# Attention feeding a two-layer network: normalising and transposing of late pairs started by the network's gates, and one chunk normalised on two engines

## The chip, the cores and the metric

One core of a Trainium2 chip runs the whole program. Its engines work side by side and are tied by semaphores: TensorE (PE), VectorE (DVE), ScalarE (ACT), GpSimd (POOL), and SyncE (SP), which here only issues transfers. The metric is the device time of one execution in microseconds, as the median of several runs.

## What is computed

Causal attention by blocks of 64 positions, then a two-layer network on its output, all in float32 (cut):

```python
scores = scale * np.matmul(q, k.transpose(0, 1, 3, 2))       # 8 batches, 8 heads, 576 positions, 64 per head
scores = np.where(block_i >= block_j, scores, -1000000000.0)
attn = np.exp(scores - np.max(scores, axis=-1, keepdims=True))
attn = attn / (np.sum(attn, axis=-1, keepdims=True) + 1e-09)
x = np.matmul(attn, v)                                       # then reshaped to 4608 tokens x 512
h = x @ w_in                                                 # 512 -> 2048
return (h * (1.0 / (1.0 + np.exp(-1.702 * h)))) @ w_out      # 2048 -> 512
```

## The kernel before

**Attention.** Two heads are done together as a pair; there are 32 pairs, n = 0 to 31, four to a batch. The queries of a pair are cut into five chunks, i = 0 (64 queries) and 1 to 4 (128 each). Chunk i sees 64(2i+1) keys. For each chunk and head, `score` puts the scores in a PSUM bank (matmuls `bank<-qk` in early pairs, `bank<-high`, `bank<-high,low` and `bank<-low,high` in late ones). `weigh` adds the mask and takes the maximum on DVE (L448, `e<-bank`), then the exponential on ACT (L455), with the sum in `sm`. `normalise` makes the reciprocal on DVE (L464, L469) and multiplies `e` by it for each head, on POOL (L474), or for chunk 4 of late pairs on DVE (L476). `turn` (late pairs) transposes `e` on DVE in blocks of 32 into `turned`: the blocks left of the diagonal by one instruction a head (L483), and the diagonal blocks of both heads by one (L488, called the diagonal turn here; in the profile 64x128, in the program's order 64x2x2x32). After chunk 4's turn, 16 transfers on SP's queue put the parts of `turned` in their places (L495). `av` multiplies by the values on PE (`bank<-turned,vp`) and ACT copies the result to `xr` (L574, L575). In early pairs (n < 8) `flip` does the transposing with PE (L117) and ACT instead.

`prep` readies q and k of the next pair: two transposes on DVE (L332, to `qt` and `raw`), two roundings on ACT (L333, `high`), and the remainders on POOL (`low`, L88).

**The network.** Tokens are done in 12 tiles of 384. A tile has 16 gates. A gate is 12 matmuls into the bank `hp`, then `tanh` on ACT (`g<-hp`, L692), the product on DVE (`g<-g,hp`, L693), its rounding on ACT (`gh`, L701), and the remainder on POOL (`gl`, L88); then come the nine matmuls of the gate before it into three accumulators `acc`, six on `gh` (`woh`, `wol`) and three on `gl`. There is one buffer `g`, so the next `tanh` waits for this `gl`. At a tile's start `split` rounds `xr` to `xh` on ACT (L626) and makes `xl` on DVE. At its end ACT copies each `acc` to `osb` (L658) and issues its transfer.

**Order.** `ORDER` gives for each pair a row of slots: digits are the chunks that are scored, V is `av` of the pair before, N normalises and T turns the chunks that were weighed, L is `prep`. Matmuls of the network fill in between the slots by a quota. HANDOVER is the row of pair 8, FIRST_LATE that of pair 9. In a late pair V also scores chunk 4 of the running pair. After its weighing, `settle` calls `prep` of the next pair, and normalises and turns chunk 4. The recording layer sorts each engine's instructions; those marked with `tc.keep_in_program_order` keep their place among each other, and `tc.high_priority` draws a gate's instructions forward.

**The lent bank.** Late, gates take two PSUM banks in turn for `hp`. The one that is not in use is lent to the first score matmul of a pair and to chunk 4, and the gate behind a loan uses the same bank as the gate ahead of it:

```python
def next_hp():
    if turns["late"] and not gate_bank["lent"]:
        gate_bank["now"], gate_bank["spare"] = gate_bank["spare"], gate_bank["now"]
    gate_bank["lent"] = False
    return ps.tile([P, 512], F32, tag=gate_bank["now"], name="hp")
```

So the first score matmul of a pair, `bank<-high 64x64`, writes the bank from which the gate before the last read its `hp`.

Of the kernel before, what the change touches and what calls it, by code (L numbers as in the profile page):

```python
# [14 lines left out]
ALU = mybir.AluOpType  # L15
# [10 lines left out]
ORDER = (  # L26
# [3 lines left out]
)  # L30

START = "1+0 - B 2/3 L C - V - 4 - a - - -"
HANDOVER = "B C - 0+3/2+1 - - N - T - V - L - - -"
FIRST_LATE = "0+3/2+1 - - N - - T - - V - - -"


WEIGHTS_BY = ((0, 0), (8, 13), (14.5, 32))
# [4 lines left out]
def attention_moe_kernel(  # L42
# [9 lines left out]
    nc = tc.nc  # L52
# [20 lines left out]
    def f(ap):  # L73
        return ap.bitcast(F32)
# [115 lines left out]
    def width(i):  # L190
        return BLK * (2 * i + 1)
# [208 lines left out]
    def settle(n, banks, todo):  # L400
        for chunks, part in zip(banks, todo):
            e = {}
            for i, hd, lo, hi, s in part:
                if i not in e:
                    e[i] = es[i] if early(n) else weights_of(n, i)
                weigh(n, i, hd, lo, hi, s, e[i])
            if early(n):
                for i in chunks[::-1]:
                    if n == 2 * HP - 1 and i == NCH - 1:
                        with tc.high_priority(offset=300):  # L410
                            normalise(n, i, e[i])
                    else:
                        normalise(n, i, e[i])
            else:
                weighed.extend((n, i, e[i]) for i in chunks[::-1])
            if 4 in chunks and not early(n):
                if n + 1 < NPAIR and n != 2 * HP:
                    prep(n + 1)
                normalise_all()
                turn_all()  # L420

    weighed = []
    shared = {}

    def weights_of(n, i):
# [3 lines left out]
            shared[n] = d2.tile([P, 2, S], F32, tag="e0", name="e", bufs=1)  # L429
        return shared[n][:, :, BLK * i * i : BLK * (i + 1) * (i + 1)]  # L430

    def normalise_all():
        for x in weighed:
            normalise(*x)

    def turn_all():
        for x in weighed:
            turn(*x)
        weighed.clear()

    def weigh(n, i, hd, lo, hi, s, e):
        mx, sm = stats[n]
# [14 lines left out]
                bias=mx[0:m, i, hd : hd + 1], accum_out=sm[0:m, i, hd : hd + 1],  # L457
            )

    def normalise(n, i, e):  # L460
        _, sm = stats[n]
        m = BLK if i == 0 else P
        c = sm[0:m, i]
        x = nc.vector.tensor_scalar(  # L464
            out=c, in0=c, scalar1=1e-9, scalar2=2.0, op0=ALU.add, op1=ALU.mult
        )
        if not early(n) and i == NCH - 1:
            tc.keep_in_program_order(x)
        nc.vector.reciprocal(out=c, in_=c)  # L469
        on = SCALE_ON[phase(n)][i]  # L470
        for hd in range(2):
            x, sc = e[0:m, hd], c[:, hd : hd + 1]
            if on == "P":
                nc.gpsimd.tensor_tensor(out=x, in0=x, in1=sc.to_broadcast([m, width(i)]), op=ALU.mult)  # L474
            elif on == "D":
                nc.vector.tensor_scalar(out=x, in0=x, scalar1=sc, scalar2=None, op0=ALU.mult)  # L476
            else:
                nc.scalar.activation(out=x, in_=x, func=AF.Copy, scale=sc)

    def turn(n, i, e):  # L480

        for hd in range(2 if i else 0):
            nc.vector.transpose(  # L483
                out=tw[:, :, SLOT[i] : SLOT[i] + i, hd].rearrange("p b j c -> p j b c"),
                in_=e[:, hd, 0 : i * P],
            )
        r, half = slice(BLK, P) if i else slice(0, BLK), slice(2, 4) if i > 2 else slice(0, 2)
        nc.vector.transpose(  # L488
            out=tw[r, half, DIAG[i]].rearrange("p b h c -> p h b c"), in_=e[r, :, i * P : width(i)]
        )  # L490
        if i == NCH - 1:
            for kb in range(4):
                for qb in range(4):
                    ns = NT4 if qb > 1 else 10 if kb > 1 else 11
                    nc.sync.dma_start(  # L495
                        out=pw[kb * 32 : kb * 32 + 32, qb, 0:ns], in_=tw[qb * 32 : qb * 32 + 32, kb, 0:ns]
                    )
# [92 lines left out]
    def step(n):  # L590

        turns["n"] = n
        now = n < NPAIR

        def item(x):
            if x == "V":
                return (lambda: av(n - 1)) if n else None
            if x in ("N", "T"):
                return normalise_all if x == "N" else turn_all
            if x == "L":  # L600
                return (lambda: prep(n + 1)) if n + 1 < NPAIR else None
            if x in ("a", "B", "C"):
                m, chunks = {"a": (n, [0, 1]), "B": (n - 1, [2, 3]), "C": (n - 1, [4])}[x]
                return (lambda: flip(m, chunks)) if m >= 0 else None
            return (lambda: score(n, [[int(z) for z in y.split("+")] for y in x.split("/")])) if now and x != "-" else None

        return [item(x) for x in order(n)]
# [29 lines left out]
    def moe():  # L637
        prev = None

        def second(state):  # L640
            g_hi, g_lo, fc, acc, t = state
            todo = [(c, ga, wb) for c in range(TILES[t][1] // P) for ga, wb in ((g_hi, "woh"), (g_hi, "wol"), (g_lo, "woh"))]
            if fc < NFC - 1:

                todo.sort(key=lambda x: (fc == 0 and x[0] == 2, x[1] is g_lo))
            elif t == NT - 1:
                todo.sort(key=lambda x: (x[0] == 2, x[1] is g_lo))
            begun = set()
            for x, (c, ga, wb) in enumerate(todo):
                last = ga is g_lo  # L650
                mm(
                    out=acc[c], lhsT=ga[:, c * P : (c + 1) * P], rhs=weights(wb, fc // FG)[:, fc % FG],
                    start=fc == 0 and c not in begun, stop=fc == NFC - 1 and last,
                )
                begun.add(c)
                if fc == NFC - 1 and last:
                    osb = out_room([P, DM], F32, "osb", t == NT - 1)
                    nc.scalar.copy(out=osb, in_=acc[c])  # L658
                    r = TILES[t][0] + c * P
                    tc.keep_in_program_order(nc.scalar.dma_start(out=out[r : r + P, :], in_=osb))  # L660
                if x % 3 == 2:
                    yield 650

        for t in range(NT):
            tt = TILES[t][1]
            if t == 0:
                yield ("tile", 0)
                split(0)
            xh, xl = xs["xh"], xs["xl"]
            acc = [ps.tile([P, DM], F32, tag=f"acc{c}", name=f"acc{c}") for c in range(tt // P)]  # L670
            for fc in range(NFC):
                if t == 0:
                    convert(fc // FG * GROUP + NDC + fc % FG + 1)
                hp = next_hp()
                fs = slice(fc % FG * P, (fc % FG + 1) * P)
                terms = [(wa, xb, dc) for dc in range(NDC) for wa, xb in (("wih", xh), ("wil", xh), ("wih", xl))]
                if fc == 0:

                    terms.sort(key=lambda x: x[1] is xl)
                for cnt, (wa, xb, dc) in enumerate(terms):  # L680
                    mm(
                        out=hp[:, 0:tt], lhsT=weights(wa, fc // FG)[:, dc, fs], rhs=xb[:, dc, 0:tt],
                        start=cnt == 0, stop=cnt == 3 * NDC - 1,
                    )
                    if cnt % 3 == 2:
                        yield unit1(tt)
                g = d2.tile([P, TT], F32, tag="g", name="g", bufs=1)[:, 0:tt]
                gh = d2.tile([P, TT], F32R, tag="gh", name="gh")[:, 0:tt]
                gl = d2.tile([P, TT], F32R, tag="gl", name="gl")[:, 0:tt]

                with tc.high_priority(offset=300):
                    nc.scalar.activation(out=g, in_=hp[:, 0:tt], func=AF.Tanh, scale=1.702)  # L692
                    nc.vector.scalar_tensor_tensor(  # L693
                        out=g, in0=g, scalar=1.0, in1=hp[:, 0:tt], op0=ALU.add, op1=ALU.mult
                    )

                if fc == NFC - 1 and t + 1 < NT:
                    yield ("tile", t + 1)
                    split(t + 1)
                with tc.high_priority(offset=300):  # L700
                    nc.scalar.copy(out=gh, in_=g)  # L701
                    subtract(nc.gpsimd, gl, g, f(gh))
                yield ("gate", fc)
                if prev is not None:
                    yield from second(prev)
                prev = (gh, gl, fc, acc, t)
        yield from second(prev)
# [87 lines left out]
```

## Time and profile before

| | |
|---|---|
| runs | 1100.33, 1099.47, 1097.53 us; median 1099.47 |
| profiled execution | 1097.42 us, span 1095.6 us |
| mean granted clock of TensorE | 0.989 |
| busy PE, DVE, ACT, POOL | 1055.2, 596.1, 521.7, 477.1 us |

The page cuts the span in 40 slices of 27 us. In its second part PE's row reads 5, 8 and 6 tenths in the first three slices and 9 in nearly all later ones: the early pairs are alone at first, then the network runs with them, and from about 930 us it runs alone. A row of a timeline has the start in us, the duration in us, the engine, the line, the operation, what it writes and reads, the count of merged instructions, and in brackets the idle time before it with what ended it. A row of waits has the waiting engine and line, what released it, the total in us, how often, and the longest. A row of windows has the stretch, its length, the busy time of PE, weight loads, DVE, ACT and POOL, the granted clock, and the transfers' share.

### The profile page before, as it was taken

What the parts mean: (1) busy time and instruction counts of PE and PEld (TensorE: products, weight loads), DVE (VectorE), ACT (ScalarE), POOL (GpSimd) and SP (SyncE); (2) the same over time, 40 slices, a digit from 0 to 9 for tenths busy, and PEclk for the clock granted to TensorE, in tenths of its full rate; (3) what the DMA queues carried; (4) which work ended last, traced back from release to release, by engine and by line L of the source; (5) the groups of instructions that cost most, each with busy time, mean ns of one, the idle gap of its engine ahead of it and who ended that gap; (6) DMA issues with size and microseconds to landing.
All of it is one profiled execution on the core that took longest, in us unless ns stands there. A gap on an engine that the chain in (4) does not pass through costs nothing. (4 is left out here: it accounts for less than half of the span.)

```text
span 1095.6 us, 20658 instructions
## 1 busy us (share of the span) xinstructions
PE 1055.2 (96%) x7236; PEld 920.8 (84%) x7236; DVE 596.1 (54%) x1856; ACT 521.7 (48%) x1367; POOL 477.1 (44%) x601
## 2 busy tenths in 40 slices
PE   5869999999999999999999999999999999999998
PEld 3657777888888888898888888888888888999987
DVE  6786786745654655655646655645665654211111
ACT  5866776534534544444544543543544443322322
POOL 4665565634444443444444434444444343222222
PEclk8979999999999999999999999999999999999999
DMA  9634523333334443333444343333444332200000
GB/s 181 202 91 156 145 66 81 95 59 82 101 78 87 104 102 65 87 84 72 106 87 89 84 104 63 81 93 78 107 98 89 65 82 49 56 29 1 30 1 30
DMA packets 222441, 92.08 MB, mean 84 GB/s; under 512 B 200832, under 2 KB 200832, under 8 KB 222336
## 3 DMA queue, kind: packets, MB, share of 16 engines
q1 hardware_dynamic: 212416, 80.73, 32.6%
q10 hardware_dynamic: 9920, 10.03, 2.6%
q8 instruction: 57, 0.93, 0.4%
q14 instruction: 48, 0.39, 0.1%
HBM read 45.88 MB, written 9.44 MB: 50 GB/s over the span
## 5 line engine op out<-in xcount | busy, mean ns | idle before, releaser
L88 POOL TENSOR_TENSOR gl<-g,gh 128x384 fp32r<-128x384 f32 x192 | 194.2, 1012 | 440.6 <-ACT gh L701 434.5
L693 DVE SCALAR_TENSOR_TENSOR g<-g,hp 128x384 f32<-128x384 f32 x192 | 105.3, 548 | 359.8 <-ACT g L692 359.7
L114 PE MATMUL hp<-xh,wih 128*128 128x384 f32 x768 | 261.1, 340 | 3.1 <-DVE g L693 2.4
L114 PE MATMUL hp<-xh,wil 128*128 128x384 f32 x768 | 258.7, 337 | 0.0
L114 PE MATMUL hp<-xl,wih 128*128 128x384 f32 x768 | 255.1, 339 | 0.1
L114 PE MATMUL acc<-woh,gh 128*128 128x512 f32 x576 | 232.0, 403 | 4.0 <-ACT gh L701 4.0
L114 PE MATMUL acc<-wol,gh 128*128 128x512 f32 x576 | 227.2, 394 | 0.0
L692 ACT ACTIVATE g<-hp 128x384 f32<-128x384 f32 x192 | 93.5, 487 | 250.3 <-PE hp L114 187.6
L701 ACT CAST gh<-g 128x384 fp32r<-128x384 f32 x192 | 98.5, 513 | 175.9 <-DVE g L693 175.0
L114 PE MATMUL acc<-woh,gl 128*128 128x512 f32 x576 | 170.6, 394 | 3.1 <-POOL gl L88 3.1
L114 PEld LDWEIGHTS hp<-xh,wih 128*128 128x128 f32 x768 | 144.6, 188 | 16.2 <-DVE g L693 3.3
L114 PEld LDWEIGHTS hp<-xh,wil 128*128 128x128 f32 x768 | 144.6, 188 | 7.7
L114 PEld LDWEIGHTS hp<-xl,wih 128*128 128x128 f32 x768 | 144.0, 188 | 1.4 <-DVE xl L88 1.4
L455 ACT ACTIVATE e<-e,mx 128x192 f32<-128x192 f32 (+3 forms) x240 | 132.4, 554 | 6.4 <-DVE mx L448 4.9
L114 PEld LDWEIGHTS acc<-woh,gl 128*128 128x128 f32 x576 | 107.3, 188 | 30.4 <-POOL gl L88 6.7
L114 PEld LDWEIGHTS acc<-woh,gh 128*128 128x128 f32 x576 | 108.1, 188 | 26.9 <-ACT gh L701 4.6
L474 POOL TENSOR_TENSOR e<-e,sm 128x448 f32<-128x448 f32 (+1 forms) x192 | 112.4, 612 | 35.4 <-DVE sm L469 22.4
L114 PEld LDWEIGHTS acc<-wol,gh 128*128 128x128 f32 x576 | 108.4, 188 | 17.0 <-issue 0.4
L448 DVE CUSTOM_DVE_ANT_0 e<-bank,mask 128x192 f32<-128x192 f32 (+3 forms) x240 | 93.2, 440 | 7.2 <-PE bank L114 7.0
L114 PEld LDWEIGHTS bank<-turned,vp 128*64 128x64 f32 (+1 forms) x1800 | 79.3, 136 | 13.8 <-issue 10.8
L114 PE MATMUL bank<-turned,vp 128*64 128x128 f32 (+2 forms) x1800 | 87.5, 259 | 1.6 <-ACT turned L509 1.6
L483 DVE STREAM_TRANSPOSE turned<-e 128x384 f32<-128x384 f32 (+1 forms) x192 | 84.0, 484 | 0.9 <-issue 0.2
(62 smaller groups left out, 1181.0 us busy)
## 6 DMA issues: line engine op xcount, KB each, us to landing
turned<-turned SPq DMA_DIRECT2D x192, 96.0 KB, 2.2
raw<-in_q_dram SPq DMA_DIRECT2D x128, 72.0 KB, 2.3
out_dram<-osb ACTq DMA_DIRECT2D x36, 256.0 KB, 2.4
raw<-in_k_dram SPq DMA_DIRECT2D x120, 72.0 KB, 2.4
turned<-turned SPq DMA_DIRECT2D x96, 88.0 KB, 2.1
words<-in_moe_w_in_dram SPq DMA_DIRECT2D x16, 512.0 KB, 6.0
vp<-in_v_dram SPq DMA_DIRECT2D x60, 128.0 KB, 2.6
turned<-turned SPq DMA_DIRECT2D x96, 80.0 KB, 2.1
```

What stands on the lines that cost most here:

```text
L88: eng.tensor_tensor(out=out, in0=in0, in1=in1, op=ALU.subtract)
L114: return tc.keep_in_program_order(nc.tensor.matmul(**kw))
L448: nc.vector.tensor_tensor_reduce(out=e[0:m, hd, lo:hi], in0=s, in1=mk, op0=ALU.add, op1=ALU.min, scale=-0.125, scalar=3e38 if lo == 0 else ...
L455: nc.scalar.activation(out=e[0:m, hd], in_=e[0:m, hd], func=AF.Exp, scale=-1.0, bias=mx[0:m, i, hd : hd + 1], accum_out=sm[0:m, i, hd : hd ...
L474: nc.gpsimd.tensor_tensor(out=x, in0=x, in1=sc.to_broadcast([m, width(i)]), op=ALU.mult)
L483: nc.vector.transpose(out=tw[:, :, SLOT[i] : SLOT[i] + i, hd].rearrange("p b j c -> p j b c"), in_=e[:, hd, 0 : i * P],)
L692: nc.scalar.activation(out=g, in_=hp[:, 0:tt], func=AF.Tanh, scale=1.702)
L693: nc.vector.scalar_tensor_tensor(out=g, in0=g, scalar=1.0, in1=hp[:, 0:tt], op0=ALU.add, op1=ALU.mult)
L701: nc.scalar.copy(out=gh, in_=g)
```

## The change

Before, N normalised all weighed chunks at one place and T turned them at another. Now N only notes how many there are (`begin_pace`). From then on each gate, right behind its remainder `gl`, normalises up to two chunks (`gate_scales`), and the next gate, right behind its product, turns them (`gate_turns`). What is left when chunk 4 has been weighed is done there, as before (`finish_all`). POOL's multiplications and DVE's turns that a gate hands out keep their program order. The T slots are gone. Besides, in pair 7 (the last early one) chunk 4 is normalised with head 0 on DVE and head 1 on POOL, where POOL did both. The arithmetic is the same.

```diff
@@ -26,12 +26,12 @@
 ORDER = (
     "1+0 - B 2/3 - L C - 4 - V - a -",
     "1+0 - B - 2 - C - 3 L V - a - 4 -",
-    "0+3/2+1 - N - T - - V - - - - -",
+    "0+3/2+1 - N - - - - V - - - - -",
 )
 
 START = "1+0 - B 2/3 L C - V - 4 - a - - -"
-HANDOVER = "B C - 0+3/2+1 - - N - T - V - L - - -"
-FIRST_LATE = "0+3/2+1 - - N - - T - - V - - -"
+HANDOVER = "B C - 0+3/2+1 - - N - - - V - L - - -"
+FIRST_LATE = "0+3/2+1 - - N - - - - - V - - -"
 
 
 WEIGHTS_BY = ((0, 0), (8, 13), (14.5, 32))
@@ -416,10 +416,11 @@
             if 4 in chunks and not early(n):
                 if n + 1 < NPAIR and n != 2 * HP:
                     prep(n + 1)
-                normalise_all()
-                turn_all()
+                finish_all()
 
     weighed = []
+    scaled = []
+    pace = {"left": 0}
     shared = {}
 
     def weights_of(n, i):
@@ -429,14 +430,37 @@
             shared[n] = d2.tile([P, 2, S], F32, tag="e0", name="e", bufs=1)
         return shared[n][:, :, BLK * i * i : BLK * (i + 1) * (i + 1)]
 
-    def normalise_all():
+    def pin(ins, behind):
+
+        if behind:
+            tc.keep_in_program_order(ins)
+
+    def finish_all():
+
+        pace["left"] = 0
         for x in weighed:
             normalise(*x)
-
-    def turn_all():
-        for x in weighed:
+        for x in scaled + weighed:
             turn(*x)
+        scaled.clear()
         weighed.clear()
+
+    def begin_pace():
+        pace["left"] = len(weighed)
+
+    def gate_turns():
+
+        for x in scaled:
+            turn(*x, behind=True)
+        scaled.clear()
+
+    def gate_scales():
+
+        for x in weighed[: min(2, pace["left"])]:
+            normalise(*x, behind=True)
+            weighed.remove(x)
+            scaled.append(x)
+            pace["left"] -= 1
 
     def weigh(n, i, hd, lo, hi, s, e):
         mx, sm = stats[n]
@@ -457,7 +481,7 @@
                 bias=mx[0:m, i, hd : hd + 1], accum_out=sm[0:m, i, hd : hd + 1],
             )
 
-    def normalise(n, i, e):
+    def normalise(n, i, e, behind=False):
         _, sm = stats[n]
         m = BLK if i == 0 else P
         c = sm[0:m, i]
@@ -470,24 +494,26 @@
         on = SCALE_ON[phase(n)][i]
         for hd in range(2):
             x, sc = e[0:m, hd], c[:, hd : hd + 1]
+            if n == 2 * HP - 1 and i == NCH - 1:
+                on = "DP"[hd]
             if on == "P":
-                nc.gpsimd.tensor_tensor(out=x, in0=x, in1=sc.to_broadcast([m, width(i)]), op=ALU.mult)
+                pin(nc.gpsimd.tensor_tensor(out=x, in0=x, in1=sc.to_broadcast([m, width(i)]), op=ALU.mult), behind)
             elif on == "D":
                 nc.vector.tensor_scalar(out=x, in0=x, scalar1=sc, scalar2=None, op0=ALU.mult)
             else:
                 nc.scalar.activation(out=x, in_=x, func=AF.Copy, scale=sc)
 
-    def turn(n, i, e):
+    def turn(n, i, e, behind=False):
 
         for hd in range(2 if i else 0):
-            nc.vector.transpose(
+            pin(nc.vector.transpose(
                 out=tw[:, :, SLOT[i] : SLOT[i] + i, hd].rearrange("p b j c -> p j b c"),
                 in_=e[:, hd, 0 : i * P],
-            )
+            ), behind)
         r, half = slice(BLK, P) if i else slice(0, BLK), slice(2, 4) if i > 2 else slice(0, 2)
-        nc.vector.transpose(
+        pin(nc.vector.transpose(
             out=tw[r, half, DIAG[i]].rearrange("p b h c -> p h b c"), in_=e[r, :, i * P : width(i)]
-        )
+        ), behind)
         if i == NCH - 1:
             for kb in range(4):
                 for qb in range(4):
@@ -595,8 +621,8 @@
         def item(x):
             if x == "V":
                 return (lambda: av(n - 1)) if n else None
-            if x in ("N", "T"):
-                return normalise_all if x == "N" else turn_all
+            if x == "N":
+                return begin_pace
             if x == "L":
                 return (lambda: prep(n + 1)) if n + 1 < NPAIR else None
             if x in ("a", "B", "C"):
@@ -694,12 +720,14 @@
                         out=g, in0=g, scalar=1.0, in1=hp[:, 0:tt], op0=ALU.add, op1=ALU.mult
                     )
 
+                gate_turns()
                 if fc == NFC - 1 and t + 1 < NT:
                     yield ("tile", t + 1)
                     split(t + 1)
                 with tc.high_priority(offset=300):
                     nc.scalar.copy(out=gh, in_=g)
                     subtract(nc.gpsimd, gl, g, f(gh))
+                gate_scales()
                 yield ("gate", fc)
                 if prev is not None:
                     yield from second(prev)
```

The instructions of PE and of SP stand in the same order in both programs. On ACT three places differ: at the start of a tile, the third copy `osb<-acc` now stands ahead of the `tanh` next to it.

DVE in an ordinary late pair, from the last reciprocal of the four chunks to the first weighing of chunk 4, before:

```order
L469 RECIPROCAL sm<-sm 128x2
L693 SCALAR_TENSOR_TENSOR g<-g,hp 128x384 x2
L488 STREAM_TRANSPOSE turned<-e 64x2x2x32 x2
L693 SCALAR_TENSOR_TENSOR g<-g,hp 128x384
L488 STREAM_TRANSPOSE turned<-e 64x2x2x32
L693 SCALAR_TENSOR_TENSOR g<-g,hp 128x384
L483 STREAM_TRANSPOSE turned<-e 128x3x4x32 x2
L488 STREAM_TRANSPOSE turned<-e 64x2x2x32
L483 STREAM_TRANSPOSE turned<-e 128x4x32 x2
L483 STREAM_TRANSPOSE turned<-e 128x2x4x32 x2
L332 STREAM_TRANSPOSE qt<-raw 128x576
L332 STREAM_TRANSPOSE raw<-raw 128x576
```

The same place in the changed program, whose lines have moved (L719 is the product of L693; L509 and L514 are the turns of L483 and L488):

```order
L493 RECIPROCAL sm<-sm 128x2
L719 SCALAR_TENSOR_TENSOR g<-g,hp 128x384 x4
L509 STREAM_TRANSPOSE turned<-e 128x3x4x32 x2
L514 STREAM_TRANSPOSE turned<-e 64x2x2x32 x2
L509 STREAM_TRANSPOSE turned<-e 128x4x32 x2
L514 STREAM_TRANSPOSE turned<-e 64x2x2x32
L509 STREAM_TRANSPOSE turned<-e 128x2x4x32 x2
L514 STREAM_TRANSPOSE turned<-e 64x2x2x32
L332 STREAM_TRANSPOSE qt<-raw 128x576
L332 STREAM_TRANSPOSE raw<-raw 128x576
```

Three diagonal turns that stood between the products of four gates now stand behind the fourth, ahead of `qt`; the large turns stand where they stood.

DVE in the last pair, from the same reciprocals, before:

```order
L488 STREAM_TRANSPOSE turned<-e 64x2x2x32
L469 RECIPROCAL sm<-sm 128x2
L464 TENSOR_SCALAR sm<-sm 128x2
L469 RECIPROCAL sm<-sm 128x2
L488 STREAM_TRANSPOSE turned<-e 64x2x2x32 x2
L693 SCALAR_TENSOR_TENSOR g<-g,hp 128x384 x2
L483 STREAM_TRANSPOSE turned<-e 128x3x4x32 x2
```

And now:

```order
L493 RECIPROCAL sm<-sm 128x2
L488 TENSOR_SCALAR sm<-sm 128x2
L493 RECIPROCAL sm<-sm 128x2
L719 SCALAR_TENSOR_TENSOR g<-g,hp 128x384 x3
L509 STREAM_TRANSPOSE turned<-e 128x3x4x32 x2
L514 STREAM_TRANSPOSE turned<-e 64x2x2x32 x2
```

The three diagonal turns ahead of the first product have gone behind the third. The same holds for pair 9, where `qt` and one more product stand between them and the turns of chunks 1 and 2.

POOL in an ordinary late pair, before, with `e` the scaling of chunks 3, 0, 1 and 2:

```order
L88 TENSOR_TENSOR low<-qt,high 128x288 x2
L88 TENSOR_TENSOR gl<-g,gh 128x384 x2
L474 TENSOR_TENSOR e<-e,sm 128x448 x2
L474 TENSOR_TENSOR e<-e,sm 64x64 x2
L474 TENSOR_TENSOR e<-e,sm 128x192 x2
L474 TENSOR_TENSOR e<-e,sm 128x320 x2
L88 TENSOR_TENSOR gl<-g,gh 128x384 x4
```

And now:

```order
L88 TENSOR_TENSOR low<-qt,high 128x288 x2
L88 TENSOR_TENSOR gl<-g,gh 128x384 x4
L500 TENSOR_TENSOR e<-e,sm 128x448 x2
L500 TENSOR_TENSOR e<-e,sm 64x64 x2
L88 TENSOR_TENSOR gl<-g,gh 128x384
L500 TENSOR_TENSOR e<-e,sm 128x192 x2
L500 TENSOR_TENSOR e<-e,sm 128x320 x2
```

The scaling has moved two gates back and is parted by a `gl`.

## The prediction

> **What bounds the kernel now.** I read, in this order, the page's busy times, the windows by stage, the waits of PE, and then the timelines of PE and DVE at the places named there.
>
> ```profile
> PE 1055.2 (96%) x7236; PEld 920.8 (84%) x7236; DVE 596.1 (54%) x1856; ACT 521.7 (48%) x1367; POOL 477.1 (44%) x601
> 300.00:910.00 610.00, 607.56 (x4310) 540.96 (x4309) 354.02 (x1148) 284.67 (x759) 270.97 (x354) 1.00 0.39 87
> PE bank L117 <- POOL turned L474: 4.1, 3, 2.9
> PE acc L114 <- ACT gh L701: 4.0, 2, 2.4
> PE acc L114 <- POOL gl L88: 3.1, 5, 0.8
> PE bank L114 <- DVE g L693: 0.2, 1, 0.2
> ```
>
> PE is busy 96% of the span, and between 300 and 910 us it is busy 607.56 of 610 at full granted clock. The change leaves PE's own order alone, so it can only remove waits of PE or add some. The waits that it can reach are few: `gh` 4.0, `gl` 3.1, and part of the 4.1 for `turned`. That caps any gain near 10 us. What it can add is not capped: a wait that recurs with every late pair comes about twenty times.
>
> **The two long waits, removed.** At the first late pair with a planned N (about 215 us) and the last pair (about 908 us), DVE has diagonal turns in front of `g`, and these wait for POOL's scaling.
>
> ```profile
> 215.15 0.47 ACT L692 ACTIVATE g<-hp 128x384 f32<-128x384 f32 x1
> 218.64 0.31 DVE L488 STREAM_TRANSPOSE turned<-e 64x128 f32<-64x128 f32 x1 [1.05 <-POOL e L474]
> 218.98 0.56 DVE L693 SCALAR_TENSOR_TENSOR g<-g,hp 128x384 f32<-128x384 f32 x1
> 220.13 0.50 PE L114 MATMUL acc<-woh,gh 128*128 128x512 f32 x1 [2.36 <-ACT gh L701]
> 912.46 0.50 PE L114 MATMUL acc<-woh,gh 128*128 128x512 f32 x1 [1.60 <-ACT gh L701]
> ```
>
> In the new order `g` stands ahead of all these turns, and the scaling comes behind two more `gl`. `g` then waits for `tanh` alone, which ends at 215.62, and can run some 3 us earlier; `gh`, which is 0.65 behind `g` and takes half a microsecond, comes almost 1 us ahead of PE's need at 217.8 (220.13 less the wait). Both waits go: 2.4 + 1.6, and 0.1 each because a matmul after a wait takes 0.50 us (the two PE rows) instead of the page's mean of 0.40. Gain 4.2 us; I keep 3.6 to 4.4.
>
> **The gl waits.** POOL scales all four chunks, eight instructions, ahead of one `gl` (six of them here).
>
> ```profile
> 375.98 2.83 POOL L474 TENSOR_TENSOR e<-e,sm 64x64 f32<-64x64 f32 x6 [0.36 <-DVE sm L464]
> 379.82 0.72 PE L114 MATMUL acc<-woh,gl 128*128 128x512 f32 x2 [0.77 <-POOL gl L88]
> PE acc L114 <- POOL gl L88: 0.8, 2, 0.6
> ```
>
> The last row is the waits of 200 to 300 us alone. There `gl` is late only through the scales, so those two go (0.8, with the longer matmuls 1.0). The three of 0.77 us (one every 250 us, at the start of a tile) lose this cause too, but output copies on ACT queue behind the same late `tanh`, and they free the accumulator that PE needs next; of these three I count 0.2 each. Together 1.6 us, bounds 0.8 to 3.4.
>
> **Chunk 4 of pair 7 on two engines.** POOL does both heads, 1.15 us each, and PE waits for each.
>
> ```profile
> 181.13 2.26 POOL L474 TENSOR_TENSOR turned<-turned,sm 128x576 f32<-128x576 f32 x2
> 182.34 0.33 PE L117 MATMUL bank<-ident,turned 128*128 128x128 f32 x1 [0.38 <-POOL turned L474]
> 183.44 1.20 PE L117 MATMUL bank<-ident,turned 128*128 128x128 f32 x9 [0.78 <-POOL turned L474]
> 182.51 0.70 DVE L248 TENSOR_SCALAR wm<-wm 128x512 uint32<-128x512 uint32 x1 [1.73 <-ACT wm L244]
> 458.67 1.51 DVE L476 TENSOR_SCALAR e<-e,sm 128x576 f32<-128x576 f32 x2
> 458.87 1.97 POOL L88 TENSOR_TENSOR low<-qt,high 128x288 fp32r<-128x288 f32 x2 [1.52 <-ACT high L333]
> ```
>
> One POOL instruction less ends POOL's half at 182.3 instead of 183.4. DVE's half costs about half a microsecond (two took 0.96 with POOL quiet, the row at 364.70 below). Side by side, both are ready at 182.3 and PE gains 1.1; one after the other, at 182.8, and it gains 0.65. The rows at 458 speak for a mutual delay: two such scales took 1.51 beside POOL's subtractions, and these took 1.97. I take 0.8. DVE is idle ahead of its next instruction, which waits for ACT until 182.51, so nothing behind the new scale on DVE is late by more than 0.3.
> [...]
>
> **What is moved in every late pair, and what it costs.** In an ordinary pair three of the four diagonal turns (L488) now stand between other gates' `g`, where DVE is idle. The new order puts all four behind the fourth `g`, ahead of `qt` and `raw`.
>
> ```profile
> 348.50 0.64 DVE L488 STREAM_TRANSPOSE turned<-e 64x128 f32<-64x128 f32 x2
> 352.40 0.31 DVE L488 STREAM_TRANSPOSE turned<-e 64x128 f32<-64x128 f32 x1
> 356.01 0.56 DVE L693 SCALAR_TENSOR_TENSOR g<-g,hp 128x384 f32<-128x384 f32 x1 [3.30 <-ACT g L692]
> 356.48 1.03 DVE L483 STREAM_TRANSPOSE turned<-e 128x384 f32<-128x384 f32 x2
> 357.52 0.31 DVE L488 STREAM_TRANSPOSE turned<-e 64x128 f32<-64x128 f32 x1
> 357.86 1.16 DVE L483 STREAM_TRANSPOSE turned<-e 128x128 f32<-128x128 f32 x4
> 358.94 0.73 DVE L332 STREAM_TRANSPOSE qt<-raw 128x576 f32<-128x576 f32 x1
> 360.57 0.67 ACT L333 CAST high<-raw 128x576 fp32r<-128x576 f32 x1 [3.46 <-DVE raw L332]
> 363.83 0.48 ACT L692 ACTIVATE g<-hp 128x384 f32<-128x384 f32 x1
> 364.70 0.96 DVE L476 TENSOR_SCALAR e<-e,sm 128x576 f32<-128x576 f32 x2
> 366.78 0.52 DVE L693 SCALAR_TENSOR_TENSOR g<-g,hp 128x384 f32<-128x384 f32 x1
> 367.75 0.24 PE L114 MATMUL bank<-high 64*64 64x64 f32 x2
> ```
>
> From 356.48 to 367.30 this is one chain without slack: turns, `qt`, `raw`, then ACT (`high`, two `xr` copies, `high`, two exponentials, `tanh`), then on DVE chunk 4's scale and turns, then `g`. ACT's row at 360.57 waits for DVE's `raw`, and `tanh` stands behind it in ACT's queue. So what is put ahead of `qt` moves the `g` at 366.78 by its full length. Who needs that `g`? The next pair's first score matmul (367.75) writes the lent bank, which is the one from which this `g` reads `hp`. `g` ends at 367.30: 0.45 us to spare. That the wait is real shows where a pair already has two more diagonal turns in the chain:
>
> ```profile
> 261.99 0.55 DVE L693 SCALAR_TENSOR_TENSOR g<-g,hp 128x384 f32<-128x384 f32 x1 [3.42 <-ACT g L692]
> 262.58 0.51 DVE L488 STREAM_TRANSPOSE turned<-e 64x128 f32<-64x128 f32 x2
> 265.57 0.73 DVE L332 STREAM_TRANSPOSE qt<-raw 128x576 f32<-128x576 f32 x1
> 273.41 0.52 DVE L693 SCALAR_TENSOR_TENSOR g<-g,hp 128x384 f32<-128x384 f32 x1
> 273.98 0.24 PE L114 MATMUL bank<-high 64*64 64x64 f32 x2 [0.17 <-DVE g L693]
> ```
>
> Here `qt` starts 3.58 us after the gate's `g`, there 2.93: 0.65 for two turns, 0.33 each. PE waited, and started 0.05 after `g` ended; so the usable slack is 0.40. Three turns more cost 3 x 0.33 = 0.98 at the least. At the most they cost 0.42 each, 1.26, since two of them now part large turns that overlap today (the two of 0.55 each at 356.48 take 1.03 together): 0.08 more each, an estimate. I take 1.1, so PE waits 1.1 - 0.4 = 0.7 per pair (0.58 to 0.86).
>
> ```profile
> L114 PE MATMUL bank<-high 64*64 64x64 f32 x40 | 4.9, 240 | 0.0
> 456.75 1.02 DVE L88 TENSOR_TENSOR xl<-xr,xh 128x384 fp32r<-128x384 f32 x1
> 457.23 1.04 PE L114 MATMUL hp<-xl,wih 128*128 128x384 f32 x4
> ```
>
> The first row counts these matmuls between 300 and 905 us: 40, two per pair, so 20 pairs, none of which waits today. In 18 of them the price is 0.7, 12.6 us. In two (458 and 708 us) a tile starts within the chain: `xl` ends at 457.77, when PE is at the last of four matmuls that read it. There the whole 1.1 falls on PE, 2.2 us. The pair at 262 us gets one turn more: 0.4. Loss 15.2 us, bounds 12.7 to 18.5. The other moved steps are covered: each half of the scaling (under the 2.83 us that six of the eight take) fits behind a `gl` and ahead of the next, since the gates there are some 4 us apart (348.50, 352.40, 356.01); by that spacing `e` is scaled about 1.7 us before DVE turns it. The DMAs of `turned` on SP's queue are issued 1.1 later and are needed only at the next pair's V, more than half of a pair's 30 us on (20 pairs in 600 us). Three times ACT puts one output copy ahead of a `tanh`, just before a V, whose matmuls hide it.
>
> **The sum.** -4.2 - 1.6 - 0.8 + 15.2 = +8.6 us. The profiled execution took 1097.42 us (span 1095.6 and 1.8 around it), which becomes 1106.0. The median shown, 1099.47, is 2.05 above that execution; with it I forecast 1108.1 us, 0.8% slower. A change under 0.3% (3.3 us) can't be told from none here.
>
> **Rivals.**
> - Faster: the chain does not reach PE, because the delay is taken up before the `g` at 366.78. That needs a total shift of at most 0.4 us. Then the gains stand alone: 1099.5 - 6.6 = 1092.9. For it: the 18 matmuls wait for nothing today. Against it: 0.33 per turn is read in the same chain, and at 273.98 the wait appears with two turns more. Chance 0.10.
> - No change: the turns overlap better than taken, as the two at 262.58 that took 0.51 together (0.26 each). Shift 0.8: 18 x 0.4 + 2 x 0.8 + 0.3 = 9.1, less 6.6, is +2.5: 1102.0. Chance 0.11.
> - Slower still: the turns of chunks 1 and 2 wait for POOL's scaling, since it now comes a gate before them. They have about 1.7 us to spare; each microsecond beyond costs 20 us: 1128 for one. Against it, POOL has nothing else between those gates. Chance 0.05.
> - The forecast: 0.74, own range 1104 to 1113.
>
> The range 1101 to 1113 takes in the no-change case and leaves the outer two. Slower 0.79, same 0.11, faster 0.10.
>
> **What the new profile would show.** Right: about 18 waits of PE on DVE's `g` at `bank<-high 64x64`, 0.5 to 0.9 us each, with `g` at that place some 1.1 us later after its pair's V; two waits on `xl`; no wait of PE for `gh` over 1 us; at most one short wait on POOL near 182 us. Wrong: no waits on `g`, and PE busy over 608 of 610 us in the late pairs. I would be most wrong if the distance from the fourth `g` to `qt` did not grow from 2.9 to about 4 us, or if waits on POOL's scaling appeared ahead of DVE's turns.

## The result: 1.2% slower

| | before | after |
|---|---|---|
| median | 1097.69 us (6 runs, 1096.58 to 1100.33) | 1111.9 us (6 runs, 1108.52 to 1113.73) |
| profiled execution, its span | 1097.42, 1095.6 | 1112.06, 1110.3 |
| mean granted clock | 0.989 | 0.989 |

The ratio is 1.0123 (95% interval 1.0102 to 1.0144): 14.2 us by the medians and 14.7 by the spans, where the sum gave 8.6. The forecast of 1108.1 us is only 3.8 below the median of 1111.9, but 1.8 of that nearness is luck: it was counted from 1099.47, the median of the first three runs of before, and all six give 1097.69. First the page's busy times, the window of the late pairs, three rows of PE's waits, and the group of the matmul that was to wait, from 300 to 930 us (its last column is the idle time ahead of it), all of the changed kernel:

```profile
PE 1057.0 (95%) x7236; PEld 919.9 (83%) x7236; DVE 590.2 (53%) x1857; ACT 521.1 (47%) x1367; POOL 477.7 (43%) x600
300.00:910.00 610.00, 590.75 (x4192) 523.08 (x4191) 337.54 (x1101) 271.95 (x724) 261.38 (x338) 1.00 0.38 85
PE bank L114 <- DVE g L719: 16.6, 19, 2.3
PE hp L114 <- ACT xh L652: 2.8, 2, 1.4
PE acc L114 <- ACT osb L684: 1.1, 3, 0.4
L114 PE MATMUL bank<-high 64*64 64x64 f32 x40 | 5.0, 244 | 16.0 <-DVE g L719 16.0
```

PE is busy 590.75 us of 610 in the late pairs, where it was 607.56. The waits on `gh` and `gl` are gone from the table of waits; in their place PE waits 16.6 us on DVE's `g` at the first score matmul, nineteen times (18 of them, 16.0 us, within the last row's window). One ordinary pair, DVE and then PE:

```profile
353.59 0.56 DVE L719 SCALAR_TENSOR_TENSOR g<-g,hp 128x384 f32<-128x384 f32 x1 [3.64 <-ACT g L718]
354.06 1.03 DVE L509 STREAM_TRANSPOSE turned<-e 128x384 f32<-128x384 f32 x2
355.11 0.64 DVE L514 STREAM_TRANSPOSE turned<-e 64x128 f32<-64x128 f32 x2
356.15 0.31 DVE L514 STREAM_TRANSPOSE turned<-e 64x128 f32<-64x128 f32 x1
357.26 0.31 DVE L514 STREAM_TRANSPOSE turned<-e 64x128 f32<-64x128 f32 x1
357.60 0.78 DVE L332 STREAM_TRANSPOSE qt<-raw 128x576 f32<-128x576 f32 x1
365.48 0.52 DVE L719 SCALAR_TENSOR_TENSOR g<-g,hp 128x384 f32<-128x384 f32 x1
366.06 0.24 PE L114 MATMUL bank<-high 64*64 64x64 f32 x2 [0.66 <-DVE g L719]
```

From the fourth `g` to `qt` it is now 4.01 us (357.60 less 353.59), where it was 2.93: all four diagonal turns stand there. The `g` that ends the chain ends at 366.00, and PE, which has been ready for 0.66, starts at 366.06.

Because PE runs the same instructions in the same order in both programs, the start of one matmul in both traces tells how far the changed kernel is behind at that place. What happens between two places is what the difference grows or shrinks by:

| matmul | before | after | after less before |
|---|---|---|---|
| second flip of chunk 4, pair 7 | 183.44 | 182.07 | -1.4 |
| first `woh,gh` after the first long wait | 220.13 | 216.27 | -3.9 |
| first score matmul near 262 to 274 | 273.98 | 269.72 | -4.3 |
| the next one (a tile has begun in that pair) | 305.54 | 302.38 | -3.2 |
| an ordinary one | 367.75 | 366.06 | -1.7 |
| `hp` of a tile that starts within the chain | 456.88 | 457.96 | +1.1 |
| first score matmul, a tile has begun | 555.76 | 560.65 | +4.9 |
| `hp` of a tile that starts within the chain | 706.98 | 716.25 | +9.3 |
| behind the scores of a pair in which a tile has begun | 807.90 | 821.95 | +14.1 |
| last pair's first score matmul | 900.49 | 916.96 | +16.5 |
| first `woh,gh` behind the second long wait | 912.46 | 927.16 | +14.7 |

### The profile page after: what moved, and what is told of

It is laid out like the page before. It is cut to its first block, busy times and chain, and to the rows that moved or that the text cites. A ratio compares the mean times of both kernels' runs of the same rounds, so it can differ in the third digit from the quotient of the medians.

```text
span 1110.3 us, 20530 instructions
## 1 busy us (share of the span) xinstructions
PE 1057.0 (95%) x7236; PEld 919.9 (83%) x7236; DVE 590.2 (53%) x1857; ACT 521.1 (47%) x1367; POOL 477.7 (43%) x600
## 4 chain that ended last, share of the span: by engine, by line
PE 68%; DVE 14%; ACT 9%; DMA 4%; issue 3%; POOL 1%; SPq 1%; DVEq 0%; ACTq 0%; POOLq 0%
PE hp L114 27%; PE acc L114 27%; PE bank L114 12%; DVE turned L509 4%; ACT e L479 3%; DMA vp<-in_v_dram 2%; DVE e L502 1%; ACT high L333 1%; DVE g L719 1%; DVE sm L488 1%; DVE turned L514 1%; DMA out_dram<-osb 1%; ACT turned L479 1%; PE bank L117 1%; DVE wm L259 1%
## 5 line engine op out<-in xcount | busy, mean ns | idle before, releaser
L719 DVE SCALAR_TENSOR_TENSOR g<-g,hp 128x384 f32<-128x384 f32 x192 | 105.4, 549 | 379.1 <-ACT g L718 379.0
L509 DVE STREAM_TRANSPOSE turned<-e 128x384 f32<-128x384 f32 (+1 forms) x192 | 85.6, 482 | 0.7 <-issue 0.3
```

What stands on the lines that cost most here:

```text
L509: pin(nc.vector.transpose(out=tw[:, :, SLOT[i] : SLOT[i] + i, hd].rearrange("p b j c -> p j b c"), in_=e[:, hd, 0 : i * P],), behind)
L719: nc.vector.scalar_tensor_tensor(out=g, in0=g, scalar=1.0, in1=hp[:, 0:tt], op0=ALU.add, op1=ALU.mult)
```

## The experiments

The theory is the prediction's: what stands on DVE between the fourth `g` and `qt` reaches PE through the lent bank. Its rival is POOL: that the scaling, handed out later, is what makes things late. For the three pairs with far longer waits (1.5 to 2.3 us, beside 0.66) the changed kernel's trace suggested a second cause, the output copy on ACT.

**1. Lending another bank.** Every engine runs the same instructions in the same order as in the changed kernel; only the bank that a gate last read is given to the fourth scores of a pair instead of the first.

```diff
-  ss.append(lent_bank() if taken == 1 and turns["late"] else bank())
+  ss.append(lent_bank() if taken == 4 and turns["late"] else bank())
```

> The changed kernel, but the lent bank goes to the fourth bank of a pair's scores and not to the first; the instructions of all engines stand in the same order, only the banks differ. Theory (PE waits because the first score matmul writes the bank from which g still reads): the bank is written some 0.9 us later, the waits of 0.65 us vanish, the three large ones shrink by 0.9, those on xh stay: 1112 - 16 x 0.73 - 2.7 - 0.4 = about 1097. Rival (PE would wait there anyway, for scores' inputs or weights that come late with the same chain): another wait of the same length appears in its place, 1112.

Measured: 1097.6 us (ratio to before 1.000, 0.9991 to 1.0009), 14.3 less than the changed kernel. The same group, from 250 to 930 us, of this kernel:

```profile
L114 PE MATMUL bank<-high 64*64 64x64 f32 x42 | 5.1, 240 | 0.0
```

So the waits at the first score matmul (16.0 us in all in the changed kernel's row) come from its write to the bank from which `g` reads: DVE's order is that of the changed kernel, and PE no longer waits there. The rival's second wait did not appear in the ordinary pairs. What is left of waits on `g` from 295 to 920 us of this kernel:

```profile
PE bank L114 <- DVE g L719: 1.7, 3, 1.0
PE hp L114 <- DVE g L719: 1.7, 3, 0.6
```

The first are the three longer pairs, at the fourth bank, which 0.9 us more could not cover; the second are three new ones at the `hp` of a gate (368, 622 and 876 us).

**2. Diagonal turns released.** The changed kernel, with the diagonal turns alone free to be moved by the recording layer:

```diff
-        pin(nc.vector.transpose(
+        nc.vector.transpose(
             out=tw[r, half, DIAG[i]].rearrange("p b h c -> p h b c"), in_=e[r, :, i * P : width(i)]
-        ), behind)
+        )
```

> The changed kernel, with only the diagonal turns released from program order, so that in an ordinary late pair three of them stand ahead of the fourth g again and one behind it; POOL, ACT and PE keep the order of the changed kernel, scaling handed out by the gates included. Theory (the diagonal turns in the chain to the lent bank are what costs): the distance from the fourth g to qt goes from 4.0 back to 2.9 us, the waits of 0.65 us vanish, the three large ones shrink by 1.0 each, the two on xh by 1.3: 1112 - 11.7 - 3.0 - 2.6 = about 1094.5. Rival (the scaling on POOL, handed out later, is what costs): nothing changes, 1112.

Measured: 1115.39 us (1.0165, 1.0145 to 1.0186), slower than the changed kernel; both numbers were missed. ACT, DVE, POOL and PE in an ordinary pair of this kernel:

```profile
352.50 0.49 ACT L718 ACTIVATE g<-hp 128x384 f32<-128x384 f32 x1 [2.06 <-PE hp L114]
353.90 0.31 DVE L514 STREAM_TRANSPOSE turned<-e 64x128 f32<-64x128 f32 x1 [1.05 <-POOL e L500]
354.24 0.55 DVE L719 SCALAR_TENSOR_TENSOR g<-g,hp 128x384 f32<-128x384 f32 x1
357.17 0.74 DVE L332 STREAM_TRANSPOSE qt<-raw 128x576 f32<-128x576 f32 x1
351.54 2.33 POOL L500 TENSOR_TENSOR e<-e,sm 128x192 f32<-128x192 f32 x4
365.58 0.24 PE L114 MATMUL bank<-high 64*64 64x64 f32 x2 [0.75 <-DVE g L719]
```

The distance from the fourth `g` to `qt` did return to 2.93. But the diagonal turns of chunks 1 and 2 now stand ahead of that `g` and wait there for POOL, whose scaling of these chunks ends at 353.87; the `tanh` was done at 352.99 (its start at 352.50 and 0.49). So `g` starts 1.2 us late, about what the three turns had cost. The rival's mechanism is real too: with the scaling handed out this late, the turns of chunks 1 and 2 can't come before the fourth `g`. That left open whether those of chunks 3 and 0 can.

**3. The first turns put ahead of the fourth `g`.** The changed kernel, where the first `g` behind handed-out turns is queued behind them on DVE, which the recording layer does not do by itself (it takes `g` first):

```diff
         for x in scaled:
-            turn(*x, behind=True)
+            last_turn[:] = [turn(*x, behind=True)]
...
+                    with tc.issue_after(last_turn.pop().ins) if last_turn else ExitStack():
                         nc.vector.scalar_tensor_tensor(
```

> The changed kernel, with the product g of the gate behind the first handed-out turns put behind them on DVE: the turns of chunks 3 and 0 (1.7 us) then run in the idle time ahead of the fourth g and not behind it. Theory (what stands between the fourth g and qt goes to PE in full, beyond 0.4 us of slack): the distance from the fourth g to qt falls from 4.0 to about 2.5 us, the waits of 0.65 us and those on xh vanish, of the three large ones 0, 0.6 and 0.5 are left: 1112 - 11.7 - 4.8 - 3.0 - 0.4 = about 1092. Rival (as with the diagonal turns released: the turns now wait for POOL's scaling, with g behind them): POOL's scaling of chunks 3 and 0 ends only 0.25 us ahead of the place where they are turned; each microsecond that it is late costs 20 us: 1112 or more.

Measured: 1091.49 us (0.9948, 0.9934 to 0.9962). An ordinary pair of this kernel:

```profile
347.82 1.03 DVE L511 STREAM_TRANSPOSE turned<-e 128x384 f32<-128x384 f32 x2
348.86 0.64 DVE L516 STREAM_TRANSPOSE turned<-e 64x128 f32<-64x128 f32 x2
351.54 0.55 DVE L723 SCALAR_TENSOR_TENSOR g<-g,hp 128x384 f32<-128x384 f32 x1 [2.03 <-ACT g L721]
353.97 0.78 DVE L332 STREAM_TRANSPOSE qt<-raw 128x576 f32<-128x576 f32 x1
PE bank L114 <- DVE g L723: 1.1, 2, 0.7
PE hp L114 <- ACT xh L655: 2.8, 2, 1.4
```

The same four turns now run while DVE would be idle; `qt` follows `g` by 2.43 us, and of 16.6 us of waits on `g` 1.1 are left, in two of the three longer pairs. One part was wrong: the two waits on `xh` stayed, of which experiment 6 tells.

**4. The output copy.** The changed kernel, with the third output copy behind the `tanh` in the three tiles where the change had put it ahead; DVE and POOL as changed.

```diff
+                    if c == 2 and t in (1, 4, 7):
+                        late_put.append(put)
+                    else:
+                        put()
...
+                    th = nc.scalar.activation(out=g, in_=hp[:, 0:tt], func=AF.Tanh, scale=1.702)
+                while late_put:
+                    with tc.issue_after(th.ins):
+                        late_put.pop()()
```

> The changed kernel, with the third output copy of three tiles (those near 288, 546 and 804 us) put behind the tanh again, as in the kernel before; ACT then has the order of before, DVE, POOL and PE that of the changed kernel. Theory (the copy waits for a transfer to free its buffer, and tanh waits behind it): the three waits of 1.5 to 2.3 us shrink to 0.65 as in ordinary pairs, 4.0 us less or 5.4 with the slow matmuls behind the third: 1106.5 to 1108. Rival (these pairs are longer because V itself or the start of the tile delays g): the waits stay, 1112.

Measured: 1106.94 us (1.0083, 1.0067 to 1.0098), less than the changed kernel by 5.0 (medians) or 4.4 us (the two ratios to before). Between the same matmuls of the two profiles it is 5.6 us, of which 1.4 is the slower TensorE behind the third wait (told at the end). First ACT at one of these places in the changed kernel, and PE at the end of the chain; then ACT here, and PE's row of waits on `g`, 12.0 us where it was 16.6:

```profile
547.18 0.59 ACT L684 COPY osb<-acc 128x512 f32<-128x512 f32 x1 [3.11 <-DMA out_dram<-osb]
547.66 0.50 ACT L718 ACTIVATE g<-hp 128x384 f32<-128x384 f32 x1
560.65 0.24 PE L114 MATMUL bank<-high 64*64 64x64 f32 x2 [2.28 <-DVE g L719]
```

```profile
545.54 0.49 ACT L725 ACTIVATE g<-hp 128x384 f32<-128x384 f32 x1 [1.97 <-PE hp L114]
546.33 0.58 ACT L687 COPY osb<-acc 128x512 f32<-128x512 f32 x1 [0.30 <-DMA out_dram<-osb]
PE bank L114 <- DVE g L730: 12.0, 18, 0.9
```

There are two buffers `osb`, so the third copy waits for the first one's transfer to land (3.11 us in the first row); `tanh`, whose `hp` PE had finished, waited behind it. Behind the `tanh` the copy waits the same way, 0.30 us here, and holds up nothing that is late. Both together (3 and 4):

> As the run before, and the third output copy of three tiles behind the tanh. Theory: the last of the three large waits go too, 1.1 us less than turns_ahead: about 1091, which is the time of before less the three gains (4.2, 1.7 and 0.7). If the copy cost only beside the long chain: the same as turns_ahead.

Measured: 1090.44 us (0.9943, 0.993 to 0.9956), 1.05 less than turns_ahead by the medians, as expected, though two medians of five runs can't separate 1 us. With the lent bank moved as well:

> turns_ahead_copy with the lent bank given to the fourth bank of the scores as well. Theory: no wait on g at the lent bank is left to remove, so it adds nothing: the same as turns_ahead_copy within 0.2%. If the chain is still without slack in some pairs: 1 to 3 us less.

Measured: 1092.03 us (0.9946, 0.9933 to 0.9959): no change to be told from turns_ahead_copy, as expected.

**5. The gains alone.** The kernel before, with the gates handing out only in pair 9 (`2 * HP + 1`), where the first long wait stands, and in the last, and chunk 4 of pair 7 on two engines. The prediction and the text below call pair 9 the first with a planned N, though the row of pair 8 has one too. Cut to the choice of the pairs:

```diff
             if x in ("N", "T"):
+                if n in (2 * HP + 1, NPAIR - 1):
+                    return begin_pace if x == "N" else None
                 return normalise_all if x == "N" else turn_all
```

> The kernel before, with scaling and turns handed out by the gates in two pairs alone, the first with a planned N and the last, and chunk 4 of pair 7 on two engines; all other pairs as before. Theory (the long waits of 2.4 and 1.6 us go through the change in these two pairs, and it is the other pairs that lose): 1097.7 - 4.2 - 0.7 = 1092.8, the gl waits of 3.1 in all left as before. Rival (the loss sits in the handing out itself wherever it is done, or the long waits come back elsewhere): 1097 or more.

Measured: 1091.36 us (0.9952, 0.9939 to 0.9965). No wait on `gh` is left, the five `gl` waits are as before (3.1 us). The gain is 6.3 where 4.9 were expected; at the two places the trace shows 2.5 and 1.8, with 0.9 for chunk 4 5.2 in all, so the rest isn't theirs (executions differ in their first 90 us, see the end). Chunk 4 of pair 7 alone, on the kernel before:

```diff
+            if n == 2 * HP - 1 and i == NCH - 1:
+                on = "DP"[hd]
```

> The kernel before, with chunk 4 of pair 7 alone normalised on two engines. If the two halves run side by side, PE gets past its two waits near 182 us 0.7 to 1.1 us earlier and all behind it moves by as much: 1096.6 to 1097.0 against 1097.7 of before. If the engines exclude one another (POOL's half starts only when DVE's ends), 0.65. Rival, that the shortened start of the changed kernel was chance: no change, 1097.7, and two waits of PE on POOL there as before.

Measured: 1096.92 us against 1097.64 (0.999, 0.9979 to 1.0001). That is 0.7 by the medians of 11 and 21 runs, but the interval takes in 1. The trace tells more. PE in before, at the matmul ahead of the first wait, and then here, at the same matmul and at the one behind the second wait (183.44 in before):

```profile
181.56 0.40 PE L114 MATMUL acc<-wol,gh 128*128 128x512 f32 x1
```

```profile
180.41 0.40 PE L114 MATMUL acc<-wol,gh 128*128 128x512 f32 x1
181.40 1.20 PE L117 MATMUL bank<-ident,turned 128*128 128x128 f32 x9 [0.48 <-POOL turned L476]
```

One wait of 0.48 us on POOL stands where there were two, of 0.38 and 0.78. From the one matmul to the other it was 1.88 us and is 0.99: 0.89 gained, and the changed kernel gains the same there.

**6. The two pairs whose tile starts within the chain.** Changed kernel, with the old N and T in these two pairs (n = 16 and 24) only (cut to the choice of the pairs):

```diff
-            if x == "N":
-                return begin_pace
+            if x in ("N", "T"):
+                if n in (16, 24):
+                    return normalise_all if x == "N" else turn_all
+                return begin_pace if x == "N" else None
```

> The changed kernel, but in the two pairs whose tile starts within the chain (near 458 and 716 us) scaling and turns stand as in the kernel before. Theory (there the three turns, and POOL's scaling that now runs beside xl on DVE, push the last xh by 1.6 us): the two waits on xh of 1.4 us go, with the slow matmul behind them 1.56 each: 1111.9 - 3.1 = 1108.8. Rival (the tile's start itself makes these waits, wherever the turns stand): unchanged, 1111.9.

Measured: 1108.88 us (1.0112, 1.0097 to 1.0127), and no wait on `xh`. The medians give 3.0, as expected, the ratios to before only 1.2, with intervals of 1.6 us and more to each side. Between the same matmuls of this profile and the changed kernel's, 3.2 us are gained at the two places. It was tried again where less else waits. The same edit on the kernel of 3 and 4 together:

> turns_ahead_copy, with the same two pairs as in the kernel before. There the turns that were put ahead of g come behind three xl and ahead of g, and the waits on xh stayed at 1.4 us. Theory: they go, 2 x 1.5 us: 1090.4 - 3.0 = 1087.4 (0.9% under before). Rival: the waits on xh have no part of these turns, 1090.4.

Measured: 1087.52 us (0.9913, 0.9896 to 0.9929), the fastest of all; the edit is worth 2.9 by the medians, 3.3 by the ratios, and again 3.2 at the two places of the profiles. Its window of the late pairs:

```profile
300.00:910.00 610.00, 609.45 (x4323) 543.60 (x4322) 346.24 (x1143) 286.15 (x758) 269.52 (x351) 1.00 0.38 87
```

PE is busy 609.45 of 610 us, so at most 0.6 us more is to be had there by moving work of the other engines.

## Why the prediction was right in kind and 6 us short

By its own steps, with what the two traces show at each:

| term | forecast | measured (from the starts of the same matmul) |
|---|---|---|
| two long `gh` waits | -4.2 | -2.5 and -1.75 |
| `gl` waits | -1.6 | -1.8: -0.8 and -0.35 in 200 to 300 us, -0.2 at each of three tiles |
| chunk 4 of pair 7 | -0.8 | -0.9 |
| pair at 262 us | +0.4 | +0.4 |
| ordinary pairs, 0.7 each | +10.5 for 15 | +11.6 (0.71 to 0.98 each) |
| three pairs in which a tile has begun, 0.7 each | +2.1 | +7.0 (1.45, 2.3, 3.3) |
| two pairs on `xl`, 1.1 each | +2.2 | +3.1 (1.56 each) |
| sum | +8.6 | +15.2 |

The remaining -0.5 lies ahead of 180 us, where nothing was changed.

The long waits went as worked out. PE at the first of them, in the changed kernel:

```profile
216.10 0.33 PE L114 MATMUL hp<-xl,wih 128*128 128x384 f32 x1
216.27 0.39 PE L114 MATMUL acc<-woh,gh 128*128 128x512 f32 x1
```

`woh,gh` follows `hp` without a gap and takes 0.39 us, where it took 0.50 behind a wait of 2.36. The `gl` waits went too, and at the three tile starts the copies kept PE waiting instead (`osb`, 1.1 us in all): 0.2 gained each, as counted. The count of the new waits was right (18 and the pair at 262 make the 19 of the table), and so were the slack of 0.40 and the shift of 1.1: the shift measured 1.08 (4.01 less 2.93).

**The step that failed** is the sentence "Three times ACT puts one output copy ahead of a `tanh`, just before a V, whose matmuls hide it." V hides a late `gh` from PE: no wait of PE on `gh` is left from 200 to 930 us. But that `tanh` makes the fourth `g`, which heads the chain of turns, `qt` and exponentials, and DVE waits for it whatever PE does (5.26 us ahead of the `g` at 548.19). The copy's own wait was not asked after: it needs a buffer whose transfer is under way, and waited 2.3 to 3.1 us. Experiment 4 puts 4.4 to 5.6 us on this. In the table the three pairs cost 4.9 more than forecast, the largest part of the 6, and 1.4 of it is the slower TensorE behind the third wait.

**A smaller one** is `xl`. The shift there was taken as the turns alone, 1.1. But POOL's second half of the scaling now runs just when DVE makes three `xl`:

```profile
448.66 1.63 DVE L88 TENSOR_TENSOR xl<-xr,xh 128x384 fp32r<-128x384 f32 x3 [1.50 <-ACT xh L626]
450.46 0.55 DVE L693 SCALAR_TENSOR_TENSOR g<-g,hp 128x384 f32<-128x384 f32 x1 [0.17 <-ACT g L692]
```

```profile
449.45 0.49 ACT L718 ACTIVATE g<-hp 128x384 f32<-128x384 f32 x1 [0.24 <-PE hp L114]
448.18 2.46 DVE L88 TENSOR_TENSOR xl<-xr,xh 128x384 fp32r<-128x384 f32 x3 [1.84 <-ACT xh L652]
447.94 3.27 POOL L500 TENSOR_TENSOR e<-e,sm 128x192 f32<-128x192 f32 x4
450.56 0.54 DVE L719 SCALAR_TENSOR_TENSOR g<-g,hp 128x384 f32<-128x384 f32 x1
457.96 0.45 PE L114 MATMUL hp<-xh,wih 128*128 128x384 f32 x1 [1.41 <-ACT xh L652]
```

The first two rows are of before, with POOL idle from 448.47 to 451.64; the others are of the changed kernel. Three `xl` take 2.46 instead of 1.63 us, and the scaling 3.27 instead of the 2.33 that the same chunks took in experiment 2, so the `g` behind `xl` starts at 450.56 although its `tanh` was done at 449.94. The wait came on the last `xh` (ACT makes it behind `raw`), earlier than the `xl` that the forecast named. Experiment 6 returns about 3 us, which is the part of these pairs; how that divides between the turns and the longer `xl` is read from these rows alone, since no run parts the two. Just ahead the changed kernel is 0.48 us early (430.62 against 431.10), so without delay this `g` would start at 449.98: it is 0.58 late. With 1.08 for the turns that makes 1.66, an estimate, where 1.56 was measured.
The kernel of experiment 3 shows it again: there three `xl` took 2.46 us from 443.10 and the same scaling 3.27 from 442.87. Beside each other `xl` took 0.83 us more and the scaling 0.94.

**Chunk 4 of pair 7** was taken at 0.8, between 0.65 (one engine after the other) and 1.1 (side by side). In the changed kernel DVE's half takes 0.79 us and POOL's 1.37, with 1.13 for one before:

```profile
180.21 0.79 DVE L502 TENSOR_SCALAR turned<-turned,sm 128x576 f32<-128x576 f32 x1
180.64 1.37 POOL L500 TENSOR_TENSOR turned<-turned,sm 128x576 f32<-128x576 f32 x1
182.07 1.20 PE L117 MATMUL bank<-ident,turned 128*128 128x128 f32 x9 [0.48 <-POOL turned L500]
```

The two overlap by 0.36 us (180.64 to 181.00), and POOL's is 0.24 longer than one of before. The gain of 0.89 is one POOL half of 1.13 less these 0.24. It lies between the two, and 0.8 was close; DVE's half began 0.43 us ahead of POOL's, where the forecast had them start together. The rows don't show whether POOL waited for these 0.24 us or ran slower.

Of the rivals, "slower still" (turns that wait for POOL's scaling) did not occur in the changed kernel, but experiment 2 shows how near it stood: moved one place ahead, turns wait 1.05 us in the pair shown. "Faster" fell with the slack, which was there for 0.4 us and no more, and "no change" with the shift, which was 1.08 and not 0.8.

## What to carry to other kernels

Work that is moved out of idle gaps is free only as long as it stands outside the chain that some engine has no slack on; look for that chain's head (here a product on DVE that no busy share points to, and behind which 1.08 us more cost PE 0.71 to 0.98 in each ordinary pair) and ask of everything queued ahead of it, on every engine, what that thing itself waits for. A resource that is lent, such as the bank here, ties the borrower to the lender's last reader: lending it to a later user took back 14.3 of the 22 us that the table counts as losses, without moving one instruction. And an order that a recording layer sorts by its own estimates has to be read back after each edit: the turns "handed out" to a gate came behind the next gate's product, and one ordering edge there turned 1.2% slower into 0.5% faster.

## What was not expected of the hardware

After one of the three long waits TensorE ran slower for about 3 us. Window and matmuls at 818 us of the changed kernel, and the window behind the wait at 560:

```profile
819.00:823.00 4.00, 4.00 (x28) 3.58 (x29) 2.04 (x10) 2.23 (x6) 1.87 (x2) 0.60 0.65 147
818.83 0.32 PE L114 MATMUL bank<-high 64*64 64x64 f32 x2 [2.16 <-DVE g L719]
819.17 0.72 PE L114 MATMUL bank<-high 64*128 64x448 f32 x2
560.85 0.45 PE L114 MATMUL bank<-high 64*128 64x448 f32 x2
560.00:563.00 3.00, 2.35 (x27) 2.11 (x28) 1.11 (x4) 1.00 (x2) 1.02 (x1) 1.00 0.71 136
```

The granted clock averages 0.60 over these 4 us: it was 0.50 up to about 822.2 us and 1.00 behind. The same matmuls took 0.72 instead of 0.45 us, and the delay grew by another 1.4 us (from the first score matmul to `woh,gh` it was 3.12 us, 818.83 to 821.95, where before took 1.74, 806.16 to 807.90); behind the longer wait of 2.28 us at 560 the clock stayed at 1.00. So of two waits of like length, 2.16 and 2.28 us, a slower clock followed the shorter alone; what decides it is not shown.

Programs that are alike up to there also differ in their first 90 us from one execution to the next: one matmul of the network's first tile starts at 85.74 us in the profiled execution of before and at 85.14 in the changed kernel's, and one just ahead of chunk 4 of pair 7 at 181.02 and 180.53, and in split_only (chunk 4 of pair 7 alone) at 179.86, though nothing that PE waits for is changed ahead of them. That is as large as several terms of the sum, and is why terms were measured between two places of one trace, and not from the ends.
